# One row of w spread by a matrix product, second paths for three steps, and a new written order of all tasks

## The chip, the cores and the metric

The kernel runs on one core of one Trainium2 chip. A core has five engines that run side by side, each through its own instruction list in order: TensorE (PE, matrix products and transposes into PSUM), VectorE (DVE), ScalarE (ACT), GpSimd (POOL) and SyncE (SP, which here only issues DMAs). The metric is the device time of one execution in microseconds (us); lower is better. Three runs of the kernel before gave 139.99, 140.60 and 140.88 us, so the median is 140.60.

## The reference, cut to what matters

Two stages follow each other. The first is a linear attention with a decay `w` per head and channel and a bonus `u` for the token itself; its output is the input `x` of the second, which rotates `x` by an angle, mixes along the tokens, and then along the channels. There are B = 4 batches, H = 8 heads, S = 768 tokens and D = 48 channels a head, so x has 384 columns.

```python
for t in range(S):                                   # r, k, v: (B, H, S, D);  w, u: (H, D)
    cur = einsum('bhd,bhe->bhde', u[None] * kt, vt)
    y[:, :, t] = einsum('bhd,bhde->bhe', rt, state + cur)
    state = w[None, :, :, None] * state + einsum('bhd,bhe->bhde', kt, vt)
x = y.transpose(0, 2, 1, 3).reshape(B, S, H * D)
theta = x @ w_theta
y = einsum('ts,bsd->btd', w_tok_r, x * cos(theta)) + einsum('ts,bsd->btd', w_tok_i, x * sin(theta))
u = x + y
return u + maximum(u @ w_ch, 0)                      # (4, 768, 384) float32
```

## The kernel before, in words

Each batch is cut into three groups of 256 tokens, so there are twelve groups, g = 0 to 11 (g = 3 b + pr). `front(b)` holds the first stage and the angle for the three groups of a batch, `mixing(b)` the mixing along the tokens and channels; `setup` makes constants, and `weights` brings in the four weight matrices.

A group of `front` does the following. It loads k, r and v (L426, L432). It multiplies k and r by powers of w (tasks *kw* and *rw*, L539 and L541); those powers, `rpow` and `kpow`, are made once in `setup` by an Exp (L381) of the logarithm of w (L374). PE transposes both (*flip TK*, *flip TR*, L477, eight blocks of 128x128 each) and ACT or DVE copies the result from PSUM (*out TK*, *out TR*, L492 or L493). PE multiplies the two into scores (L585), four banks of 128x512 a group; DVE multiplies each by a 0/1 mask on its way out of PSUM (*mAT*, L594). The bonus goes by *PD* (L601), *diag* (L618), *dg* (L623) and *yd* (L627). The running state of a batch goes by *outer* (L651), then *F*, *T* and *N* (L693 to L707), with bf16 copies *Sb*. PE adds up *states*, *outputs* and *bonus* (L727, L740, L756; L779 and L792 in the last groups) and the result is copied to *x* (L764, L766, L801). *TX* transposes x, *theta* is a product of it with `w_theta` (L815), ACT takes cos and sin (L822, L826), and DVE multiplies x with both into *z* (L830). Groups 0 to 6 (`PAIRS`) hold two neighbouring tokens to a partition, groups 7 to 11 one.

A group of `mixing` has two halves t. Each half is three *mix* steps of four products (L852), one for each group of z in the batch; *un* adds x to the sum (L870, DVE, PSUM to SBUF); *TU* transposes it; *chan* is the product with `w_ch` (L884); *fin out* takes the positive part (ACT, L890, with *fin add* on POOL, L897, or DVE in one step, L893); SP writes the result out (L908, L903). The token weights must be transposed before any *mix*: POOL issues six casting loads (L446; *Wr* and *Wi* casts 0 to 2), each followed by two flips of six blocks, *flip Wr0* to *Wr5* and *flip Wi0* to *Wi5*; cast 1 feeds flips 2 and 3, cast 2 feeds flips 4 and 5. Output rows of half t in pair pr of a batch need the flips number 2 pr + t of both.

All of these are *tasks* of a `Plan`. A task lists the engines on which it can run (its *ways*), and the set of lists at the top of the file decides everything else: `ORDER` is the order in which tasks are issued, and so the order within each engine and DMA queue; `WAYS` picks each task's way; `BANKS` gives the PSUM bank of every product; `AFTER` adds ten waits of one task for another; `IDLE` puts matrix products with a zero tile, whose result nobody reads, behind a task (`unread`, L284). Such products also stand at the start (`WARM`: 6 and 8). Data dependencies are waited for besides. A transpose with a second way can be done by a DMA from SP (L483), and then its copy from PSUM falls away (way `NONE`).

At the start the tile of w, 128 equal rows, is read by one DMA of ACT (L293: `in_=rows_of(w, C)`), small tiles of w and u by two more (L388). PE's order begins: 14 zero products, the transpose of the small tile (*wu flip*, L395), flip TR0, flip TK0, flip TK2, and so on; DVE copies the small tile (*wup*, L400) before its first multiplication by a power.

Of the kernel before, what the change touches and what calls it, by code (L numbers as in the profile page):

```python
# [951 lines left out]
```

## Time and profile before

| what | value |
|---|---|
| three runs | 139.99, 140.60, 140.88 us; median 140.60 |
| profiled execution, first to last instruction (span) | 138.9 us |
| median of the runs less that span | 1.7 us |
| PE busy | 127.6 us (92%) |
| DVE, ACT, POOL busy | 107.5, 76.7, 61.7 us |
| DMA | 25.65 MB moved, 185 GB/s in the mean |

The profile gives no time of its own for the profiled execution besides the span, so sums below are made against 138.9 us, and the 1.7 us between it and the median are taken as what lies around it. A row of the view by windows shows a stretch, its length, the busy time and count of each engine, the granted TensorE clock (1.00 is full), the share of DMA and what it moved. A row of the timeline shows start, duration, engine, line, operation, what it writes and reads, and, in brackets, how long its engine had been idle and what ended that. A row of the view of DMAs ends with the time from issue to landing.

### The profile page before, as it was taken

Reading aid. Unit: us, or ns where it says so; the run is one execution under the profiler, and the core shown is the slowest. Engines: PE = TensorE matmul, PEld = TensorE weight load, DVE = VectorE, ACT = ScalarE, POOL = GpSimd, SP = SyncE. Lnnn points to the kernel's source line nnn. Section 1 sums busy time; section 2 is a strip of 40 time slices with the busy share of each in tenths; the row PEclk is TensorE's granted clock in tenths of the full one; section 3 lists DMA queues with packets and bytes.
Section 4 is the critical chain, followed back from the end, with each engine's and each line's share of the span. In section 5 each row is a group of like instructions: output and inputs, shape, how many; then the busy total and the mean of one; then the engine's idle time right before and its main releaser. Section 6 shows DMA issues by size and latency. Waiting matters only on the chain.

```text
span 138.9 us, 4469 instructions
## 1 busy us (share of the span) xinstructions
PE 127.6 (92%) x1874; PEld 85.0 (61%) x1874; DVE 107.5 (77%) x205; ACT 76.7 (55%) x145; POOL 61.7 (44%) x70
## 2 busy tenths in 40 slices
PE   0999569999996999999999999999999999999990
PEld 0334347977764767777766687577565665656640
DVE  2419397889799999999979997999699986427281
ACT  2455687799992368593898039629903133650020
POOL 5003977861041099949320199993118902002000
PEclk9999985799999999999999999999999999999999
DMA  2999999999999999739979999999972563803635
GB/s 46 250 263 263 261 225 213 210 239 211 248 254 267 261 196 147 107 67 174 193 127 267 169 217 185 147 269 187 288 177 60 103 181 87 257 0 115 114 122 218
DMA packets 67340, 25.65 MB, mean 185 GB/s; under 512 B 61816, under 2 KB 67320, under 8 KB 67320
## 3 DMA queue, kind: packets, MB, share of 16 engines
q1 hardware_dynamic: 64720, 22.22, 75.6%
q0 software_dynamic: 2432, 2.95, 12.4%
q10 hardware_dynamic: 168, 0.20, 0.7%
q8 instruction: 14, 0.23, 0.7%
q14 instruction: 6, 0.05, 0.1%
HBM read 20.25 MB, written 4.72 MB: 180 GB/s over the span
## 4 chain that ended last, share of the span: by engine, by line
PE 65%; DVE 10%; DMA 8%; POOL 6%; SPq 4%; issue 2%; ACT 2%; DVEq 0%; ACTq 0%; POOLq 0%
PE bank L852 25%; PE bank L477 9%; DMA ld<-in_v_dram 8%; PE bank L815 6%; PE bank L884 5%; PE bank L284 5%; PE bank L585 4%; POOL Kw L539 3%; PE bank L651 2%; SPq L432 2%; PE bank L740 2%; DVE Rw L539 2%; DVE PD L601 2%; PE bank L756 1%; PE bank L792 1%
## 5 line engine op out<-in xcount | busy, mean ns | idle before, releaser
L852 PE MATMUL bank<-z,WrT 128*128 128x384 bf16 x144 | 46.8, 326 | 0.0
L852 PE MATMUL bank<-z,WiT 128*128 128x384 bf16 x144 | 46.8, 326 | 0.0
L594 DVE TENSOR_TENSOR mAT<-bank,mask 128x512 bf16<-128x512 f32 x28 | 18.1, 681 | 4.3 <-PE bank L585 4.1
L539 POOL TENSOR_TENSOR Kw<-ld,kpow 128x768 bf16<-128x768 f32 x4 | 8.2, 2040 | 24.5 <-DVE Kw L539 9.9
L852 PEld LDWEIGHTS <-WrT 128*128 128x128 bf16 x144 | 14.0, 98 | 8.1
L852 PEld LDWEIGHTS <-WiT 128*128 128x128 bf16 x144 | 14.1, 98 | 8.0
L870 DVE TENSOR_TENSOR uu_all<-bank,x 128x384 bf16<-128x384 f32 x24 | 13.0, 549 | 4.9 <-PE bank L852 4.7
L826 ACT ACTIVATE trig<-bank 128x384 f16<-128x384 f32 x24 | 11.4, 504 | 7.9 <-PE bank L815 7.8
L627 POOL TENSOR_TENSOR yd<-dg,vb 128x768 bf16<-128x768 f32 x10 | 14.7, 1470 | 2.3 <-ACT lwu L403 1.3
L492 ACT ACTIVATE RT<-bank 128x1024 bf16<-128x1024 bf16 x11 | 11.3, 1026 | 6.8 <-PE bank L477 6.6
L884 PE MATMUL bank<-Wch,uu_all 128*128 128x384 bf16 x72 | 14.6, 326 | 0.1
L897 POOL TENSOR_TENSOR fin_all<-fin_all,uu_all 128x384 f32<-128x384 f32 x8 | 7.3, 913 | 16.1 <-ACT fin_all L890 14.8
L815 PE MATMUL bank<-Wth,xT 128*128 128x384 bf16 x72 | 14.3, 326 | 0.0
L284 PE MATMUL bank<-zero 128*128 128x512 bf16 x31 | 10.9, 503 | 3.6 <-DVE zero L291 3.6
L822 ACT ACTIVATE trig<-bank,pi 128x384 f16<-128x384 f32 x24 | 13.6, 594 | 0.7 <-PE bank L815 0.6
L830 DVE TENSOR_TENSOR z<-x,trig 128x1536 bf16<-128x1536 bf16 x12 | 11.7, 974 | 2.9 <-ACT trig L822 2.9
L492 ACT ACTIVATE KT<-bank 128x1024 bf16<-128x1024 bf16 x11 | 11.5, 1044 | 3.3 <-PE bank L477 3.0
L594 DVE TENSOR_TENSOR mAT<-bank,mask_c 128x512 bf16<-128x512 f32 x20 | 13.0, 681 | 0.2 <-PE bank L585 0.2
L539 POOL TENSOR_TENSOR Rw<-ld,rpow 128x768 bf16<-128x768 f32 x4 | 7.2, 1812 | 8.2 <-DVE PD L601 8.1
L893 DVE SCALAR_TENSOR_TENSOR fin_all<-bank,uu_all 128x384 f32<-128x384 f32 x16 | 8.6, 551 | 2.2 <-PE bank L884 1.8
L539 DVE TENSOR_TENSOR Rw<-ld,rpow 128x768 bf16<-128x768 f32 x8 | 9.2, 1152 | 1.0 <-DMA ld<-in_r_dram 1.0
L477 PE MATMUL bank<-ident,Kw 128*128 128x128 bf16 x96 | 7.4, 219 | 2.5 <-POOL Kw L539 2.5
(112 smaller groups left out, 219.6 us busy)
## 6 DMA issues: line engine op xcount, KB each, us to landing
ld<-in_r_dram SPq DMA_DIRECT2D x12, 384.0 KB, 6.0
out_dram<-fin_all SPq DMA_DIRECT2D x11, 384.0 KB, 3.1
ld<-in_k_dram SPq DMA_DIRECT2D x7, 384.0 KB, 10.5
ld<-in_v_dram SPq DMA_DIRECT2D x7, 384.0 KB, 6.1
ld<-in_k_dram SPq DMA_DIRECT2D x10, 192.0 KB, 4.8
ld<-in_v_dram SPq DMA_DIRECT2D x10, 192.0 KB, 5.2
z<-in_moe_w_tok_i_dram POOLq DMA_DIRECT2D x1, 384.0 KB, 7.3
fin_all<-in_moe_w_tok_r_dram POOLq DMA_DIRECT2D x1, 384.0 KB, 8.4
```

The costliest lines, as they stand in the source:

```text
L284: ins = [nc.tensor.matmul(bank_t[k][:, :wide * C].rearrange("p (a c) -> p a c", a=wide), zero, bc(zero, 1, wide), start=True, stop=True, s ...
L477: ins = [nc.tensor.matmul(bank16(tok)[:, i * C:(i + 1) * C], s, ident, is_transpose=True, start=(i == 0), stop=(i == n - 1)) for i, s in e ...
L492: ways = [act(n * C, lambda: nc.scalar.activation(dst, src(), Act.Copy)), dve(n * C, lambda: nc.vector.tensor_copy(dst, src()), 1.0 if pai ...
L539: return eng.tensor_mul(to.rearrange("p j h d -> p h j d")[:, :, :, :D], tokens(i), pw)
L594: mask01[:, j] if pairs else mask_c): nc.vector.tensor_mul(
L627: return eng.tensor_mul(yd.rearrange("p a b d -> p (a b) d"), wide(dg, D), vb.rearrange("p a b d -> p (a b) d"))
L815: ins = [nc.tensor.matmul(bank(th)[:, :HD], xT[:, t, dk, :], Wth[:, dk, :], start=(dk == 0), stop=(dk == ND - 1)) for dk in range(ND)]
L822: P.add(act(HD, lambda th=th, t=t, trig=trig: nc.scalar.activation(trig[:, t, 0], bank(th)[:, :HD], Act.Sin, bias=pi2), 144), use=[th], rd ...
L830: P.add(dve(4 * HD, lambda trig=trig, pr=pr: nc.vector.tensor_mul(z[:, 2 * pr:2 * pr + 2], bc(x[:, 2 * pr:2 * pr + 2], 2, 2), trig), 2.0, ...
L852: ins.append(nc.tensor.matmul(bank(tm)[:, :HD], (WrT, WiT)[ri][:, so, to * C:(to + 1) * C], z[:, so, ri], start=(part == 0 and i == 0), st ...
L870: P.add(dve(HD, lambda tm=tm, t=t, to=to, un=un: nc.vector.tensor_add(un[:, t], bank(tm)[:, :HD], x[:, to])), use=[tm], rd=[("x", xi, pr, ...
L884: ins = [nc.tensor.matmul(bank(tf)[:, :HD], uT[:, t, dk, :], Wch[:, dk, :], start=(dk == 0), stop=(dk == ND - 1)) for dk in range(ND)]
```

## The change

First, w: the DMA reads w as one row of 384 numbers into one partition. A new DVE task fills a row of 128 ones, and a new PE task, *spread*, multiplies the two, which puts w on all 128 partitions of a PSUM bank; the logarithm reads that bank. Spread stands behind the zero products of the start in PE's order, of which there are now six. Second, paths: a score tile can be copied out of PSUM by ACT and masked from SBUF to SBUF by DVE or POOL; a mixed sum can be copied by ACT and added to x by POOL; the transposes of k in groups 7 to 11 can be done by a DMA, for which their blocks are laid out in another order. Third, all lists are new.

```diff
-WARM, WARM_NS = (6, 8), (1280, 1700)
+WARM = 6
...
-    (69, 155), (125, 85), (156, 93), (168, 134), (249, 279), (215, 285), (232, 346), (454, 326),
-    (467, 586), (448, 633),
-]
...
+AFTER = []
 IDLE = [
-    (28, 0, 5), (73, 3, 5), (71, 3, 5), (83, 2, 1), (119, 0, 1),
+    (6, 2, 6), (74, 4, 2), (72, 5, 1), (121, 6, 1), (119, 4, 5), (91, 2, 1), (166, 6, 1), (99,
+    5, 3), (101, 4, 1),
 ]
...
-        P.add((ACT, 2950, False, lambda: nc.scalar.dma_start(out=w_row, in_=rows_of(w, C))),
+        P.add((ACT, 2950, False, lambda: nc.scalar.dma_start(
+            out=w_row[:1], in_=w.rearrange("h d -> (h d)").unsqueeze(0))),
...
+        P.add((DVE, 70, False, lambda: nc.vector.memset(one, 1.0)), wr=["one"], prio=-2e4,
+              name="one")
+
+        def spread():
+            a = nc.tensor.matmul(bank("wsp")[:, :HD], one, w_row[:1], start=True, stop=True)
+            return a, a
+        P.add(pe(640, spread), rd=["one", "w_row", "warmed"], acq=["wsp"], prio=-2e4, mode=5,
+              name="spread")
...
         P.add(act(HD, lambda: nc.scalar.activation(
-            lw_f, w_row, Act.Ln), 93), rd=["w_row", "set"], wr=["lw_f"], prio=-200,
-            name="ln")
+            lw_f, bank("wsp")[:, :HD].rearrange("p (h d) -> p h d", h=H), Act.Ln)),
+            use=["wsp"], rd=["set"], wr=["lw_f"], prio=-200, name="ln")
...
+                    P.add([(NONE, 0, False, None),
+                           act(HP * C, lambda hi=hi, tk=tk, mAT=mAT: nc.scalar.activation(
+                               mAT[:, hi], bank(tk[hi]).rearrange("p (h t) -> p h t", h=HP),
+                               Act.Copy))], use=[tk[hi]], wr=[("mAT", mi, hi)], prio=pb + 3,
+                          name="mA out", kind="mA")
...
+                           dve(HP * C, lambda hi=hi, mAT=mAT, m=m: nc.vector.tensor_mul(
+                               mAT[:, hi], mAT[:, hi], m), 2.0, True),
+                           pool(1170, lambda hi=hi, mAT=mAT, m=m: nc.gpsimd.tensor_mul(
+                               mAT[:, hi], mAT[:, hi], m))],
...
+                P.add([(NONE, 0, False, None),
+                       act(HD, lambda tm=tm, t=t, fin=fin: nc.scalar.activation(
+                           fin[:, t], bank(tm)[:, :HD], Act.Copy))], use=[tm],
+                      wr=[("fin", j, t)], prio=pb + 2 * t, name="un out", kind="un")
+                P.add([dve(HD, lambda tm=tm, t=t, to=to, un=un: nc.vector.tensor_add(
+                           un[:, t], bank(tm)[:, :HD], x[:, to])),
+                       pool(900, lambda t=t, to=to, un=un, fin=fin: nc.gpsimd.tensor_add(
+                           un[:, t], fin[:, t], x[:, to]))],
```

The new `ORDER`, `WAYS` and `BANKS`, 838 entries and more, are left out. Read off task by task they say the following. The numbers before the dot are the group, behind it the half.

- Of 48 score tiles, 28 stay on DVE alone; 20 are copied by ACT and then masked by DVE (14) or POOL (6). Of 24 sums, six go by ACT and POOL. Of the late transposes of k, groups 10 and 11 go by DMA. TX8 goes from PE to DMA, TU1 and TX4 from DMA to PE.
- The first loads come in the order r0, k0, r1, k1, k2, v0, r2, v1, v2, k3, r3 (before: r0, k0, k2, r1, k1, v0, v1, r2, v2, r3, k3).
- PE begins: six zero products, spread, six zero products, wu flip, TR0, two zero products, TK0, one, TR1, one, scores 0, TK1, five, scores 1.0, diag 0, scores 1.1, outer 0, one, diag 1, TK2, one, states 0, three, TR2, outputs 0.0, outer 1, outputs 0.1, one, scores 2, bonus 0, states 1, outputs 1, bonus 1, flips Wi2 and Wi3, TX0, TX1, diag 2, outer 2, theta 0 and 1, states 2, outputs 2, bonus 2, flips Wr3 and Wr2, TK3, TX2, mix 1.0.0, mix 1.1.0, theta 2.1, TR3, theta 2.0, mix 1.1.1, flip Wr4, scores 3, mix 1.0.1, flip Wi4, mix 1.1.2, flip Wi5, mix 1.0.2, flip Wr5; twenty tasks later flip Wi0.
- DVE begins: constants, rw0, wup, kw0, rw1, kw1, PD0, mask, three score tiles of group 0 with uw among them, PD1, then the rest of groups 0 and 1 with T0; a constant, F1, Sb (three), T1, yd1, a mask, PD2, out Wi2, vb2, two tiles of group 2, Sb, out Wi3, Sb, the third tile, kw3, z0.
- POOL begins: constants, kw2, Wi cast 1, Wth, rw2, N0, yd0, N1, Wr cast 1, two Sb, one score tile of group 2, yd2, Wr cast 2, Wi cast 2, rw3, kw5, the sum 1.0, Wi cast 0, Wr cast 0. (Before: kw2, Wi cast 2, Wth, kw1, Wr casts 2 and 1, yd0, N0, Wi cast 1, two Sb, yd1, Wr cast 0, N1, Wi cast 0, yd2.)
- At the end PE has the same last tasks (flip TU11.1, chan 9.1, flip TU11.0, chan 11.1, chan 11.0); chan 10.0 and 10.1 come among the last mix steps instead of behind them.

More of the change, by code (lines that the diff above doesn't have):

```diff
@@ L140, in issue @@
             if way[0] == NONE:
-                t.ins = self.tasks[seq - 1].ins
+                t.ins = next(d.ins for d in t.deps)
                 continue
@@ L215 @@
     zero = sb.tile([C, C], BF16, name="zero")
+    one = sb.tile([1, C], F32, name="one")
     col_i = sb.tile([C, C], mybir.dt.int32, name="col_i")
@@ L259 @@
     w_row, lw_f = [zs[1].rearrange("p o t n -> p (o t n)")[:, 2 * i * HD:2 * (i + 1) * HD]
-                   .bitcast(F32).rearrange("p (h d) -> p h d", h=H) for i in range(2)]
+                   .bitcast(F32) for i in range(2)]
+    lw_f = lw_f.rearrange("p (h d) -> p h d", h=H)
     fins = [fin_all[:, i] for i in range(3)]
@@ L289, in setup @@
     def setup():
-        if WARM:
-            P.add((DVE, 120, False, lambda: nc.vector.memset(zero, 0.0)), wr=["zero"],
-                  prio=-3e4, name="zero")
-        P.add((ACT, 2950, False, lambda: nc.scalar.dma_start(out=w_row, in_=rows_of(w, C))),
+        P.add((DVE, 120, False, lambda: nc.vector.memset(zero, 0.0)), wr=["zero"],
+              prio=-3e4, name="zero")
+        P.add((ACT, 2950, False, lambda: nc.scalar.dma_start(
+            out=w_row[:1], in_=w.rearrange("h d -> (h d)").unsqueeze(0))),
               wr=["w_row"], prio=-3e4, name="w_row", kind="small")
@@ L471, in weights, with flip @@
         cast(Wch, moe_w_ch.rearrange("(o p) n -> p o n", p=C), ["Wch"], 15, (1, 24, 87), "Wch")
-    def flip(dst, blocks, tok, prio, rd, wr, paired=False, turned=None):
+    def flip(dst, blocks, tok, prio, rd, wr, paired=False, turned=None, packets=48):
         n = len(blocks)
@@ L483, in flip @@
             ways.append(sp(lambda: nc.sync.dma_start_transpose(
-                out=turned[0], in_=turned[1].rearrange("p t n -> p (t n)")), 1450))
+                out=turned[0], in_=turned[1]), 1450))
         P.add(ways, rd=list(rd) + ["ident"], wr=wr, acq=[tok], prio=prio,
-              desc=(0, 48, 15.5) if turned else None, name="flip " + tok[0],
+              desc=(0, packets, 15.5) if turned else None, name="flip " + tok[0],
               kind="turn" if turned else "")
@@ L530, in front @@
             RT, KT, PD = (a.rearrange("p (h c q) -> p h c q", c=2, h=HP) for a in flat)
+            if not pairs:
+                KT = flat[1].rearrange("p (c h q) -> p h c q", c=2, h=HP)
             kR, kK, kRT, kKT = ("Rw", g % NR), ("Kw", g % NK), ("RT", g % NRT), ("KT", g % NKT)
@@ L550, in front @@
                       name=nm[0] + "w")
-            for to, Tw, nm, kT, kTT, two in ((KT, Kw, "TK", kK, kKT, pairs),
-                                             (RT, Rw, "TR", kR, kRT, True)):
-                to = to.rearrange("p h c q -> p h (c q)")
-                flip(to.rearrange("p h (t j) -> p h t j", j=2) if two else
-                     to.rearrange("p h (c q) -> p (h c) q", c=2),
-                     [Tw[:, j, 2 * hp:2 * hp + 2, :].rearrange("p h d -> p (h d)")
-                      for hp in range(HP) for j in range(2)], (nm, g), pb, [kT], [kTT],
-                     paired=two)
+            for to, Tw, nm, kT, kTT, two in ((flat[1], Kw, "TK", kK, kKT, pairs),
+                                             (flat[0], Rw, "TR", kR, kRT, True)):
+                blocks = [Tw[:, j, 2 * hp:2 * hp + 2, :].rearrange("p h d -> p (h d)")
+                          for j in range(2) for hp in range(HP)]
+                if two:
+                    flip(to.rearrange("p (h t j) -> p h t j", h=HP, j=2),
+                         [blocks[j * HP + hp] for hp in range(HP) for j in range(2)], (nm, g),
+                         pb, [kT], [kTT], paired=True)
+                else:
+                    to = to.rearrange("p (a q) -> p a q", q=C)
+                    flip(to, blocks, (nm, g), pb, [kT], [kTT], packets=64,
+                         turned=(to, Tw.rearrange("p j h d -> p (j h d)")))
             flat_v, flat_l = vbs[g % NV], Ls[iv]
@@ L592, in front, with pairwise @@
                 for hi in range(2):
[L593 to L601 removed]
+                    m = bc(mask01[:, j] if pairs else mask_c, 1, HP)
+                    P.add([(NONE, 0, False, None),
[3 more added lines that the diff above has]
+                          name="mA out", kind="mA")
+                    P.add([dve(HP * C, lambda hi=hi, tk=tk, mAT=mAT, m=m: nc.vector.tensor_mul(
+                               mAT[:, hi], bank(tk[hi]).rearrange("p (h t) -> p h t", h=HP), m)),
+                           dve(HP * C, lambda hi=hi, mAT=mAT, m=m: nc.vector.tensor_mul(
+                               mAT[:, hi], mAT[:, hi], m), 2.0, True),
+                           pool(1170, lambda hi=hi, mAT=mAT, m=m: nc.gpsimd.tensor_mul(
+                               mAT[:, hi], mAT[:, hi], m))],
+                          use=[tk[hi]], rd=["mask" if pairs else "mask_c"],
+                          wr=[("mAT", mi, hi)], prio=pb + 3, name="mAT", kind="mA")
+            def pairwise(eng, of=flat if pairs else (RT, KT, PD)):
+                return eng.tensor_mul(of[2], of[0], of[1])
             P.add([dve(1024, lambda f=pairwise: f(nc.vector), 2.0, True),
@@ L860, in mixing @@
                           name="mix")
-                if b * NCH + to in UN_BY_TWO:
-                    P.add(act(HD, lambda tm=tm, t=t, fin=fin: nc.scalar.activation(
-                        fin[:, t], bank(tm)[:, :HD], Act.Copy)), use=[tm],
-                        wr=[("fin", j, t)], prio=pb + 2 * t, name="un out")
-                    P.add(pool(900, lambda t=t, to=to, un=un, fin=fin: nc.gpsimd.tensor_add(
-                        un[:, t], fin[:, t], x[:, to])),
-                        rd=[("x", xi, pr, t), ("fin", j, t)], wr=[("un", j, t)],
-                        prio=pb + 2 * t, name="un add")
-                else:
-                    P.add(dve(HD, lambda tm=tm, t=t, to=to, un=un: nc.vector.tensor_add(
-                        un[:, t], bank(tm)[:, :HD], x[:, to])), use=[tm],
-                        rd=[("x", xi, pr, t)], wr=[("un", j, t)], prio=pb + 2 * t, name="un")
+                P.add([(NONE, 0, False, None),
[6 more added lines that the diff above has]
+                           un[:, t], fin[:, t], x[:, to]))],
+                      use=[tm], rd=[("x", xi, pr, t), ("fin", j, t)],
+                      wr=[("un", j, t)], prio=pb + 2 * t, name="un add", kind="un")
             single = g == B * NP - 1
```

47 lines of the change are left out of this document (18 added, 29 removed), and 86 rows, old and new, of the table ORDER.

## The prediction

> **What bounds the kernel now.** I read the page's busy times first, then the view by windows cut where PE's state changes, then PE's waits, the chain of waits and the timeline of the start.
>
> ```profile
> PE 127.6 (92%) x1874; PEld 85.0 (61%) x1874; DVE 107.5 (77%) x205; ACT 76.7 (55%) x145; POOL 61.7 (44%) x70
> L284 PE MATMUL bank<-zero 128*128 128x512 bf16 x31 | 10.9, 503 | 3.6 <-DVE zero L291 3.6
> 0.00:11.00 11.00, 7.38 (x21) 2.56 (x22) 3.75 (x25) 4.44 (x7) 2.07 (x12) 1.00 0.80 190
> 11.00:19.77 8.77, 6.25 (x123) 4.14 (x123) 5.83 (x14) 5.96 (x7) 7.21 (x6) 0.99 1.26 256
> 19.77:26.30 6.53, 6.53 (x134) 4.84 (x133) 5.51 (x11) 4.90 (x13) 4.25 (x7) 0.50 1.19 211
> 26.30:35.34 9.04, 9.00 (x211) 6.92 (x210) 7.89 (x15) 8.33 (x17) 3.96 (x5) 1.00 1.15 220
> 35.34:43.00 7.66, 6.57 (x73) 4.58 (x71) 6.76 (x8) 7.10 (x13) 2.08 (x1) 1.00 1.08 257
> 43.00:131.70 88.70, 88.39 (x1301) 60.19 (x1302) 74.06 (x130) 45.00 (x88) 42.11 (x41) 1.00 0.85 167
> ```
>
> From 43 us to the tail PE is busy for 88.39 of 88.70 us, so nothing off PE is worth anything there unless it makes PE wait. The time to be had lies ahead of the first mix step at 35.34 us. Up to there PE was busy for 7.38 + 6.25 + 6.53 + 9.00 = 29.2 us, of which 10.9 us are zero products, and the stretch at clock 0.50 did half of what it could (about 2.9 us lost on real work). So 15.4 us of useful work took 35.3 us. The rows show two more losses: 1.1 us of idle PE in the window from 35.34, and the clock.
>
> **The change part by part.** *The start.* The late links of before are here (timeline, then landings in windows of issue):
>
> ```profile
> 5.55 0.52 ACT L374 ACTIVATE z<-z 128x384 f32<-128x384 f32 x1 [1.82 <-DMA z<-in_w_dram]
> 9.77 0.16 DVE L400 COPY wup<-bank 128x4 f32<-128x4 f32 x1 [4.69 <-PE bank L395]
> 9.85 0.96 DVE L539 TENSOR_TENSOR Rw<-ld,rpow 128x768 bf16<-128x768 f32 x1
> 16.60 1.82 POOL L539 TENSOR_TENSOR Kw<-ld,kpow 128x768 bf16<-128x768 f32 x1
> 18.48 0.62 PE L477 MATMUL bank<-ident,Kw 128*128 128x128 bf16 x8 [1.69 <-POOL Kw L539]
> 5.54 1.23 SPq L426 DMA_DIRECT2D ld<-in_r_dram  x1
> ld<-in_r_dram SPq DMA_DIRECT2D x1, 384.0 KB, 5.7
> z<-in_w_dram ACTq DMA_DIRECT2D x1, 192.0 KB, 4.8
> ```
>
> Before, rw0 sits behind wup, which sits behind wu flip and 14 zero products; kw1 runs on POOL, behind kw2 and two casts, and TK1 waits for it until 18.48. After, rw0 stands ahead of wup, and kw1 is DVE's, right behind rw1. kw1 then waits only for its load, the fourth: before, the fourth was issued at 5.54 and landed 5.7 later, at 11.2. The 192 KB of w, moved at the 256 GB/s of the second window, leave the queue, which is 0.77 us: 10.5. Spread is not shown; its price on the logarithm lies between a bf16 row of the same width (0.33, the mean of the mix products) and the 4.8 us that the old DMA took. I take about 1, nearer the product, since the old logarithm began at 5.55 and the new one may begin after the table load: either way the powers are there well before the fourth load. If w lands late, each us goes on rw0.
>
> *DVE then sets the pace.* Its order from kw1 is known, and its durations are these:
>
> ```profile
> L594 DVE TENSOR_TENSOR mAT<-bank,mask 128x512 bf16<-128x512 f32 x28 | 18.1, 681 | 4.3 <-PE bank L585 4.1
> L601 DVE TENSOR_TENSOR PD<-RT,KT 128x1024 bf16<-128x1024 bf16 x10 | 7.2, 720 | 0.3 <-ACT RT L492 0.3
> L703 DVE TENSOR_TENSOR T<-bank,F 128x192 f32<-128x192 f32 x8 | 2.8, 353 | 0.3
> L627 DVE TENSOR_TENSOR yd<-dg,vb 128x768 bf16<-128x768 f32 x2 | 1.9, 948 | 0.0
> L493 DVE COPY WrT<-bank 128x768 bf16<-128x768 bf16 x4 | 2.2, 545 | 0.0
> L870 DVE TENSOR_TENSOR uu_all<-bank,x 128x384 bf16<-128x384 f32 x24 | 13.0, 549 | 4.9 <-PE bank L852 4.7
> 32.34 0.57 PE L740 MATMUL bank<-vb,mAT 64*128 64x48 bf16 x32
> 32.75 0.49 PE L756 MATMUL bank<-yd,place 64*128 64x384 bf16 x4
> ```
>
> From kw1 to T1: kw1 0.96, two PD 1.44, eight score tiles 5.45, six steps of T's kind 2.1, and mask, place and uw about 1.5, taken as four more of T's kind, in all 11.5: T1 ends at 22.0. On to the last DVE tile of group 2: yd1 0.95, PD2 0.72, three copies of 0.55, three tiles 2.0, three more of T's kind (two Sb, a mask) 1.0, in all 6.3: 28.3. Outputs 2 and bonus 2 take 0.9 behind it (32.34 to 33.24 in the trace): bonus 2 ends at 29.2 instead of 33.24. By then before had done two flips of 0.34 more and one theta of 0.49 less, so the new order is ahead by 4.0 - 0.7 + 0.5 = 3.8 us.
>
> *The casts give part of it back.* POOL issues Wr cast 1 only behind N1, which waits for T1.
>
> ```profile
> 18.36 0.76 POOL L446 DMA_DIRECT2D fin_all<-in_moe_w_tok_r_dram  x1
> fin_all<-in_moe_w_tok_r_dram POOLq DMA_DIRECT2D x1, 384.0 KB, 8.4
> L627 POOL TENSOR_TENSOR yd<-dg,vb 128x768 bf16<-128x768 f32 x10 | 14.7, 1470 | 2.3 <-ACT lwu L403 1.3 <-ACT dg L623 0.7
> L706 POOL TENSOR_TENSOR N<-T,w 128x192 f32<-128x192 f32 x5 | 2.5, 500 | 2.6 <-DVE T L703 1.7 <-DVE PD L601 0.9
> L897 POOL TENSOR_TENSOR fin_all<-fin_all,uu_all 128x384 f32<-128x384 f32 x8 | 7.3, 913 | 16.1 <-ACT fin_all L890 14.8 <-ACT xT L492 1.3
> L764 ACT ACTIVATE x<-bank 128x384 bf16<-128x384 f32 x11 | 5.1, 493 | 3.7 <-PE bank L756 3.6
> 35.50 0.65 PE bank L852 x4
> 36.15 0.49 PE bank L815 x3
> 36.64 0.45 PE bank L477 x8
> 37.57 0.68 PE bank L477 x12
> 28.56 0.38 PE bank L585 x16
> ```
>
> Before, the first Wr cast was issued at 18.36; now it is at 22.0 + 0.5 = 22.5 and lands 8.4 later, at 30.9. PE stands at flip Wr3 from 29.2: 1.7 lost, 2.1 ahead. Wr cast 2 is issued behind the POOL score tile and yd2. The tile's copy stands on ACT behind x of group 1, which waits for yd1 (23.0): bonus 0.5, two x of 0.49, a copy of about 0.6, then a POOL tile of about 1.1, so 26.2; dg2 stands behind two transpose copies on ACT, near 26.9; yd2 takes 1.47; cast 2 is issued at 28.4 and lands at 36.8. PE, from 30.9, has four flips' worth of short work (0.68 + 0.45 + 0.34 + 0.45), three mix steps and two theta, 4.85 together: it stands at flip Wr4 from 35.75, 1.05 lost, 1.1 ahead. Wi cast 0 is issued behind the sum 1.0, which needs mix 1.0.2: 36.8 + three flips, two scores and three mix steps is 40.6, ACT's copy 0.49 and POOL's addition 0.91 make 42.0, and it lands 8.4 later, at 50.4. PE reaches flip Wi0 after 9.4 more of such work (five flips and six mix steps are two thirds of it), at 50.0: another 0.4. So 0.7 ahead.
>
> *Later stretches.* The idle 1.1 us of before is this:
>
> ```profile
> 40.29 2.57 DVE L539 TENSOR_TENSOR Rw<-ld,rpow 128x768 bf16<-128x768 f32 x1
> 39.96 2.08 POOL L539 TENSOR_TENSOR Kw<-ld,kpow 128x768 bf16<-128x768 f32 x1 [8.12 <-DMA ld<-in_k_dram]
> 42.91 0.62 PE L477 MATMUL bank<-ident,Rw 128*128 128x128 bf16 x8 [1.09 <-DVE Rw L539]
> ```
>
> The DVE multiplication took 2.57 beside POOL's instead of 0.96. kw6 goes to DVE, so this place goes: +1.1. TK10, TK11 and TX8 leave PE, TU1 and TX4 come back: 0.9 + 0.34 - 0.68 is +0.56. The second paths take 20 x 0.68 + 6 x 0.55 = 16.9 us from DVE and give 14 masks of 0.36 (half a PD; at most a tile's 0.68) back; but four kw, two yd, four fin out (each 0.55 like a sum), five Sb and three transpose copies come to DVE, 3.8 + 1.9 + 2.2 + 1.8 + 1.6 = 11.3, so its total falls by 16.9 - 5.0 - 11.3 = 0.6 only. A POOL tile lies between 0.98 (yd by size) and 1.47, an ACT copy between 0.49 and twice that; ACT has room beside its 76.7 us. In the tail PE's last steps are the same: 0.
>
> The 14 masks and all POOL tiles now read only SBUF, where the pair above stood in each other's way. The Trainium skill, SBUF — State Buffer, Who interferes with whom, calls the shared port of DVE and GpSimd an exclusive lock, held for a whole instruction. By that rule, with POOL busy 44% of the time, a mask would meet it about every second time and wait up to a microsecond, some 5 us more of DVE; by the sum above it is nothing, and PE's 99.7% would have to absorb it. The 2.57 us agrees with the lock.
>
> Sum: 0.7 + 1.1 + 0.5 = 2.3 us off 138.9, span 136.6; with the 1.7 us between span and median, 138.3. An unforeseen wait in the steady stretch would come off that; the old order has 0.3 us of idle PE in 88.7, so I count none.
>
> **The rivals.** *No waits on casts (G).* With less in the DMA queues at 22 us than at 18 the casts land sooner than 8.4 us, and 2.8 of the 3.15 us that the waits cost (1.7 + 1.05 + 0.4) stay: 135.5. Against it: the DMA share is over 1.0 in all windows from 11 to 43 us.
>
> *The clock falls again (C).* Before, PE was idle for 2.5 of the 8.77 us ahead of 19.77, and then the clock stood at 0.50 until 26.3. The new order waits for DVE tiles in the same stretch, with 27 zero products in all against 31. If the clock halves again while PE bounds, the same 2.9 us are lost: 138.3 + 2.9 = 141.2, no change. The Trainium skill, TensorE: Matmul & The Clock Gate, Part 4, says that transposes do not count as PE work for the gate. By that rule the eight-block transposes of the start keep nothing warm; the trace agrees only so far that the clock fell although PE was busy for 6.25 of 8.77 us.
>
> *The last casts come late (S), slower.* The last cast was issued at 28.93 before (below); now the last two stand on POOL behind an addition that needs a finished mix, and by the sum above there is no slack: every microsecond is PE's. A load that met the casts took 13.0:
>
> ```profile
> ld<-in_k_dram SPq DMA_DIRECT2D x1, 384.0 KB, 13.0
> 28.93 0.76 POOL L446 DMA_DIRECT2D x<-in_moe_w_tok_i_dram  x1
> ```
>
> 13.0 in place of 8.4 is 4.6 us: 142.9. Slower than 142.0 it is from 3.7 us on. For it: no wait of `AFTER` is kept, and order on POOL alone sets it. Against: DMA traffic may have thinned by 42 us.
>
> *It does not do what it says (N).* DVE and POOL lock each other as above and the new lists stall PE where the old did not, by as much as the casts left: 140.6.
>
> **How the numbers follow.** One per cent, 1.4 us, is about what a measurement of this kernel can tell from no change. The forecast has 0.42 and its own range, 136.5 to 139.2; G 0.14; C 0.13; N 0.12; S 0.19. Faster than 139.2: 0.42 + 0.14 = 0.56. Within 1%: C and N, 0.25. Slower: 0.19. The range reaches down into G, to 134.3, and up past C and N to 141.9, just short of S, which leaves out about two in ten.
>
> **What would show it.** In the changed profile: kw1 on DVE at 10.5 to 11.5 and TK1 before 13; T1 near 22 and bonus 2 near 29; PE idle at flips Wr3, Wr4 and Wi0 with the DMA as releaser, 1.7, 1.05 and 0.4 us; no 1.1 us idle by rw5; the window after 53 us as full as before. If PE is not idle at these flips, G holds; if the clock's slices show 5 between 14 and 26 us, C; if flip Wi0 waits 3 us or more, S; idle PE after 53 us with DVE or POOL as releaser, N. The prediction is wrong at its root if useful PE work by 35 us is not above 15.4.

## The result and the profile after

The changed kernel is slower: 145.16 us (median of four runs, 144.84 to 146.57) against 140.62 us for the kernel before, run beside it. The ratio is 1.036, with an interval of 1.030 to 1.041. The forecast was 138.3 us with a range of 134.3 to 141.9, so the sign is wrong and the time lies outside the range. Medians here and below are of all runs of a kernel, while ratios and intervals leave out runs more than 1.5% above its fastest, so the two can differ a little. The profiled execution of the changed kernel spans 143.1 us, 4.2 us more than the 138.9 of before.

The page of the changed kernel shows where to look: busy times, PE and its clock in 40 slices of 3.6 us, and the chain of waits by engine.

```profile
PE 128.6 (90%) x1862; PEld 82.9 (58%) x1862; DVE 116.2 (81%) x211; ACT 85.0 (59%) x163; POOL 60.8 (43%) x68
PE   7989797790999999896999999999999999999990
PEclk9999999999599999999999999999999999999998
PE 55%; DVE 20%; ACT 9%; DMA 7%; issue 5%; POOL 1%; POOLq 0%; DVEq 0%; ACTq 0%
```

PE is only 1.0 us busier than before, but its row has a hole (a 0 in the tenth slice, about 32 to 36 us) and behind it the clock is at half. DVE grew from 107.5 to 116.2 us, although its total was forecast to fall by 0.6. The same stretches by windows (length, busy time of PE, PEld, DVE, ACT and POOL with counts, granted clock, DMA share, GB/s):

```profile
20.00:32.28 12.28, 10.36 (x259) 7.70 (x253) 11.00 (x22) 10.20 (x20) 8.22 (x10) 1.00 1.18 258
32.28:36.06 3.78, 0.00 (x0) 0.00 (x1) 3.78 (x3) 1.26 (x2) 2.43 (x2) 0.99 1.18 218
36.06:39.40 3.34, 3.34 (x11) 1.60 (x12) 1.74 (x3) 0.00 (x0) 0.00 (x0) 0.50 1.19 284
...
53.00:135.50 82.50, 80.27 (x1122) 52.97 (x1118) 69.34 (x121) 47.22 (x96) 36.44 (x36) 1.00 0.77 158
```

Three losses stand in these rows: 1.92 us of idle PE before 32.28, 3.78 us with PE quite still and 3.34 us at clock 0.50 behind it, and 2.23 us spread over the rest (82.50 less 80.27), where the old order had 0.31 in 88.70. The timeline has the instructions, PE, DVE and POOL mixed in order of time; a bracket tells how long the engine had been idle, and for what:

```profile
10.20 0.95 DVE L552 TENSOR_TENSOR Kw<-ld,kpow 128x768 bf16<-128x768 f32 x1
21.67 0.34 DVE L728 TENSOR_TENSOR T<-bank,F 128x192 f32<-128x192 f32 x1
23.23 0.76 POOL L457 DMA_DIRECT2D uu_all<-in_moe_w_tok_r_dram  x1
25.97 0.22 PE L488 MATMUL bank<-ident,fin_all 128*128 128x128 bf16 x1 [1.81 <-issue]
30.23 0.49 PE L781 MATMUL bank<-yd,place 64*128 64x384 bf16 x4
30.40 0.72 POOL L457 DMA_DIRECT2D z<-in_moe_w_tok_i_dram  x1
30.43 5.10 DVE L855 TENSOR_TENSOR z<-x,trig 128x1536 bf16<-128x1536 bf16 x1
31.14 1.82 POOL L552 TENSOR_TENSOR Rw<-ld,rpow 128x768 bf16<-128x768 f32 x1
32.91 1.80 POOL L552 TENSOR_TENSOR Kw<-ld,kpow 128x768 bf16<-128x768 f32 x1
36.06 0.50 PE L877 MATMUL bank<-z,WrT 128*128 128x384 bf16 x1 [3.79 <-DVE WrT L504]
...
63.42 2.15 DVE L618 TENSOR_TENSOR mAT<-mAT,mask 128x512 bf16<-128x512 bf16 x1
63.79 1.49 POOL L652 TENSOR_TENSOR yd<-dg,vb 128x768 bf16<-128x768 f32 x1
67.11 0.43 PE L676 MATMUL bank<-vb,Kw 64*64 64x48 bf16 x24 [1.26 <-DVE xT L504]
```

The start went as forecast: kw1 on DVE at 10.20 (10.5 was forecast), T1 ends at 22.01 (22.0). Then PE stood for 1.81 us without any releaser ("issue"), so bonus 2 ends at 30.72 instead of 29.2. And then came the largest loss. z0, an elementwise product of two SBUF tiles that takes 0.95 us elsewhere, took 5.10 us, beside rw3 and kw5 on POOL, and ended 0.82 us behind them. The first mix step needs z0 and the copies of Wr queued behind it on DVE, so PE had nothing to do for 3.79 us, and the clock halved. At 63 us a mask of 0.41 us took 2.15 beside yd5 on POOL; PE waited 1.26 us for the copy two places behind it. Over all, by groups (busy us, mean ns):

```profile
L855 DVE TENSOR_TENSOR z<-x,trig 128x1536 bf16<-128x1536 bf16 x12 | 15.9, 1322 | 3.1 <-ACT trig L847 2.8 <-ACT trig L851 0.3
L618 DVE TENSOR_TENSOR mAT<-mAT,mask 128x512 bf16<-128x512 bf16 x7 | 5.5, 786 | 0.0
L618 DVE TENSOR_TENSOR mAT<-mAT,mask_c 128x512 bf16<-128x512 bf16 x7 | 2.9, 420 | 0.8 <-ACT mAT L612 0.8
```

In the kernel before, z took this:

```profile
L830 DVE TENSOR_TENSOR z<-x,trig 128x1536 bf16<-128x1536 bf16 x12 | 11.7, 974 | 2.9 <-ACT trig L822 2.9
```

Of the 8.7 us by which DVE grew, the products z make 4.2 (15.9 less 11.7), nearly all of it z0.

### The profile page after: what moved, and what is told of

Its sections match the earlier page's. It is cut to its first block, busy times and chain, and to the rows that moved or that the text cites. A ratio compares the mean times of both kernels' runs of the same rounds, so it can differ in the third digit from the quotient of the medians.

```text
span 143.1 us, 4466 instructions
## 1 busy us (share of the span) xinstructions
PE 128.6 (90%) x1862; PEld 82.9 (58%) x1862; DVE 116.2 (81%) x211; ACT 85.0 (59%) x163; POOL 60.8 (43%) x68
## 4 chain that ended last, share of the span: by engine, by line
PE 55%; DVE 20%; ACT 9%; DMA 7%; issue 5%; POOL 1%; POOLq 0%; DVEq 0%; ACTq 0%
PE bank L877 24%; PE bank L907 7%; DMA xT<-x 7%; PE bank L840 6%; PE bank L488 5%; DVE z L855 4%; DVE mAT L616 4%; DVE PD L626 3%; ACT RT L503 2%; DVE mAT L618 2%; PE bank L291 2%; PE bank L676 2%; PE bank L602 2%; ACT KT L503 2%; DVE Kw L552 1%
## 5 line engine op out<-in xcount | busy, mean ns | idle before, releaser
L855 DVE TENSOR_TENSOR z<-x,trig 128x1536 bf16<-128x1536 bf16 x12 | 15.9, 1322 | 3.1 <-ACT trig L847 2.8
L652 POOL TENSOR_TENSOR yd<-dg,vb 128x768 bf16<-128x768 f32 x8 | 12.1, 1516 | 11.6 <-ACT dg L648 11.6
L890 DVE TENSOR_TENSOR uu_all<-bank,x 128x384 bf16<-128x384 f32 x18 | 9.8, 551 | 7.1 <-PE bank L877 6.8
L892 POOL TENSOR_TENSOR uu_all<-fin_all,x 128x384 bf16<-128x384 f32 x6 | 6.8, 1134 | 18.2 <-ACT fin_all L887 18.2
L612 ACT ACTIVATE mAT<-bank 128x512 bf16<-128x512 f32 x20 | 11.6, 602 | 2.9 <-PE bank L602 2.8
L920 POOL TENSOR_TENSOR fin_all<-fin_all,uu_all 128x384 f32<-128x384 f32 x4 | 3.6, 912 | 18.8 <-ACT fin_all L913 18.8
L616 DVE TENSOR_TENSOR mAT<-bank,mask 128x512 bf16<-128x512 f32 x17 | 11.0, 679 | 0.1
L626 DVE TENSOR_TENSOR PD<-RT,KT 128x1024 bf16<-128x1024 bf16 x11 | 9.4, 858 | 0.5 <-ACT RT L503 0.3
L840 PEld LDWEIGHTS <-xT 128*128 128x128 bf16 x72 | 6.4, 99 | 5.6 <-DMA xT<-x 1.5
L907 PEld LDWEIGHTS <-uu_all 128*128 128x128 bf16 x72 | 6.7, 98 | 4.5 <-ACT uu_all L503 0.4
```

The costliest lines, as they stand in the source:

```text
L612: act(HP * C, lambda hi=hi, tk=tk, mAT=mAT: nc.scalar.activation(mAT[:, hi], bank(tk[hi]).rearrange("p (h t) -> p h t", h=HP), Act.Copy))] ...
L616: P.add([dve(HP * C, lambda hi=hi, tk=tk, mAT=mAT, m=m: nc.vector.tensor_mul(mAT[:, hi], bank(tk[hi]).rearrange("p (h t) -> p h t", h=HP), ...
L626: return eng.tensor_mul(of[2], of[0], of[1])
L652: return eng.tensor_mul(yd.rearrange("p a b d -> p (a b) d"), wide(dg, D), vb.rearrange("p a b d -> p (a b) d"))
L840: ins = [nc.tensor.matmul(bank(th)[:, :HD], xT[:, t, dk, :], Wth[:, dk, :], start=(dk == 0), stop=(dk == ND - 1)) for dk in range(ND)]
L855: P.add(dve(4 * HD, lambda trig=trig, pr=pr: nc.vector.tensor_mul(z[:, 2 * pr:2 * pr + 2], bc(x[:, 2 * pr:2 * pr + 2], 2, 2), trig), 2.0, ...
```

## The experiments

The theory after these rows: the new order is no worse in its work, but it puts multiplications of POOL beside those products of DVE on which PE waits, and they shut DVE out. The old order had ten waits in `AFTER`; the new one has none. Rivals: the second paths cost more than they bring; the half clock is the loss; the one-row w gives nothing; the new order is slower for other reasons. Ratios below are to the kernel before, run beside each.

| kernel | median, us | ratio (interval) |
|---|---|---|
| after | 145.16 | 1.036 (1.030 to 1.041) |
| after, two waits | 142.69 | 1.013 (1.004 to 1.022) |
| before, no waits | 144.25 | 1.027 (1.021 to 1.033) |
| after, zero products | 145.16 | 1.035 (1.027 to 1.044) |
| after, w as 128 rows | 148.29 | 1.052 (1.042 to 1.062) |
| after, two waits, one path | 145.87 | 1.040 (1.035 to 1.045) |
| after, four waits | 141.95 | 1.012 (1.007 to 1.017) |
| after, three waits | 141.41 | 1.009 (1.004 to 1.014) |
| after, two waits, late load | 141.94 | one run |
| after, three waits, late load | 139.93 | 0.996 (0.991 to 1.000) |
| before, one-row w | 138.80 | 0.991 (0.988 to 0.995) |
| before, one-row w, z2 first | 137.41 | 0.981 (0.972 to 0.991) |
| the same, kw1 on DVE | 138.01 | 0.985 (0.978 to 0.992) |

**Two waits.** rw3 starts only after z0, kw5 only after z1.

```diff
-AFTER = []
+AFTER = [(113, 207), (160, 300)]     # rw3 after z0, kw5 after z1
```

> The changed kernel with two waits put back: POOL's rw3 waits for z0, POOL's kw5 waits for z1. Lock theory: z0 took 5.10 us instead of 0.95 because rw3 and kw5 ran on POOL at that time, both engines multiplying SBUF by SBUF; with the waits z0 takes under 1.3 us, PE's idle 3.8 us ahead of the first mix step shrinks below 1 us, the clock does not fall at 36 us, and the kernel takes 139.8 to 141.2 us. Rival (cast theory): the long z0 comes from the casting load issued at 30.40, which stays: z0 stays near 5 us and the kernel near 145. Second rival (next wait): the stall goes but flip Wr4 then waits for its cast, and under 2 us is won, 143 or more.

```profile
31.22 0.96 DVE L855 TENSOR_TENSOR z<-x,trig 128x1536 bf16<-128x1536 bf16 x1 [0.74 <-ACT trig L847]
33.61 0.34 PE L877 MATMUL bank<-z,WrT 128*128 128x384 bf16 x1
```

142.69 us. z0 takes 0.96 us, PE no longer waits ahead of the first mix, and that comes 2.45 us sooner. So it was the overlap with POOL's work that made z0 late, and it cost about 2.5 of the 4.5 us that the change lost (3.2 by the ratios). In this run z0 starts when POOL is through with issuing the cast as well (30.37 to 31.09 us), so this run alone can't tell the cast from the multiplications; the kernel under "All of it", below, does. The clock fell in this run too, at 27 us, behind the stall without a releaser.

**The old kernel without its waits.** `AFTER` of before is emptied, nothing else.

```diff
-AFTER = [(69, 155), (125, 85), ..., (448, 633)]
+AFTER = []
```

> The kernel before with its ten extra waits taken out, nothing else. Lock theory: these waits kept POOL's SBUF work off DVE's; without them DVE's excess over its shortest durations grows from 2.5 us to 5 or more and the kernel loses 1 to 4 us, 141.6 to 144.6. Rival: the waits are leftovers, kw2 and its casts come earlier, and the time stays within 0.7 us of 140.6.

```profile
12.72 0.62 PE L474 MATMUL bank<-ident,Kw 128*128 128x128 bf16 x8 [1.21 <-DVE Kw L536]
17.83 0.46 PE L648 MATMUL bank<-vb,Kw 64*64 64x48 bf16 x32 [1.40 <-ACT vb L558]
29.18 0.43 PE L648 MATMUL bank<-vb,Kw 64*64 64x48 bf16 x16 [1.39 <-DVE vb L560]
39.76 1.82 POOL L536 TENSOR_TENSOR Kw<-ld,kpow 128x768 bf16<-128x768 f32 x1 [7.61 <-DMA ld<-in_k_dram]
40.52 1.87 DVE L827 TENSOR_TENSOR z<-x,trig 128x1536 bf16<-128x1536 bf16 x1
42.45 0.32 PE L849 MATMUL bank<-z,WrT 128*128 128x384 bf16 x1 [0.76 <-DVE z L827]
```

144.25 us, 4 us slower than with them: in the old order the ten waits were worth about as much as the change lost. Only a part of it is the same picture. z beside a multiplication on POOL takes 1.87 us and PE waits 0.76, and kw0 beside kw2 makes PE wait 1.21. But PE also waits 1.40 and 1.39 us for copies of v, the second of which waits for its load. And most of the loss lies in the head: from 47.00 to 135.50 us PE is idle for 1.04 us, where with the waits it was 0.31 in a stretch about as long.

**Zero products in the gap.** Fifteen products with the zero tile stand behind flip TX2, where PE waits for z0, so that the clock holds.

```diff
-    5, 3), (101, 4, 1),
+    5, 3), (101, 4, 1), (194, 6, 15),
```

> The changed kernel with 15 more zero products behind flip TX2, in the 3.8 us in which PE stood idle. The stall itself stays. Clock theory: the granted clock stays at 1.00 from 36 to 39.5 us instead of 0.50, worth half of 3.4 us: 143.4 to 143.9. Rival: the clock cost nothing because DVE was the bound there, 144.8 to 145.6.

Windows of this kernel and then of the changed one:

```profile
36.00:40.00 4.00, 3.93 (x40) 2.66 (x44) 3.26 (x6) 1.85 (x4) 0.00 (x0) 1.00 1.10 274
100.00:120.00 20.00, 18.76 (x242) 12.03 (x240) 16.00 (x30) 9.02 (x20) 6.18 (x7) 1.00 0.98 199
```

```profile
36.00:40.00 4.00, 3.94 (x20) 2.10 (x21) 1.80 (x4) 0.25 (x1) 0.00 (x0) 0.57 1.18 278
100.00:120.00 20.00, 19.82 (x249) 12.72 (x247) 16.87 (x33) 10.41 (x24) 7.77 (x9) 1.00 0.83 192
```

145.16 us, the same. The clock stayed at 1.00 (0.57 without the products) and PE did twice the instructions from 36 to 40 us, but from 100 to 120 us it now stood still for 1.24 us (20.00 less 18.76; 0.18 without). At 65 us PE was still 1.68 us ahead (65.43 against 67.11 for the same product). The half clock behind the hole is real, but removing it won nothing that these runs show: what it gave was taken back by later waits.

**w as 128 rows again.** One DMA brings 128 rows, the logarithm reads that tile, one zero product stands in place of spread; all else as changed.

```diff
-            a = nc.tensor.matmul(bank("wsp")[:, :HD], one, w_row[:1], start=True, stop=True)
-            return a, a
+            return unread(P.bank_of["wsp"], 1)
...
-            out=w_row[:1], in_=w.rearrange("h d -> (h d)").unsqueeze(0))),
+            out=w_row.rearrange("p (h d) -> p h d", h=H), in_=rows_of(w, C))),
```

> The changed kernel with w read as 128 rows again and the logarithm taken from that tile; the product that spread w is replaced by one zero product. Theory (as predicted): 192 KB more in the queue put every early load 0.77 us later, so kw1, T1 and the first mix step come 0.5 to 0.8 us later: 145.6 to 146.0. Rival: rw0 waited for the powers and not for loads, the spread took 1.6 us of PE and won nothing: 144.8 to 145.4.

```profile
7.79 0.20 PE L405 MATMUL bank<-ident_f,wu 8*128 8x8 f32 x1 [2.02 <-DMA wu<-in_w_dram]
11.29 0.96 DVE L551 TENSOR_TENSOR Kw<-ld,kpow 128x768 bf16<-128x768 f32 x1 [0.49 <-DMA ld<-in_k_dram]
```

148.29 us, 3.1 more than the changed kernel (2.3 by the ratios). I had priced the one row at 0.77 us, its bytes. PE's wait of 2.02 us for the small load of w costs nothing by itself: the flip behind it ran no later than in the changed kernel (7.79 against 7.91), and the next one needs rw0, which started 0.30 us later (7.82 against 7.52). What the 128 rows hold back is the loads of k. SP issued that of k1 at 5.55 us instead of 2.98; kw1 then waits for it and starts at 11.29 instead of 10.20, and kw2 on POOL starts at 12.91 instead of 10.62. By T1 the delay is 3.0 us (how it grew so far was not taken apart), and the first mix came at 39.35 us instead of 36.06.

**One path.** The kernel with two waits, and every mask and sum read from PSUM by DVE again, at the place of its copy.

```diff
-WAYS = (... mA out 1, mAT 1 or 2; un out 1, un 1 ...)     # 20 masks, 6 sums
+WAYS = (... mA out 0, mAT 0;      un out 0, un 0 ...)     # each product moved to its copy's place in ORDER
```

> The two-wait kernel (142.7 us) with every second path undone: all 28 mask products and all 18 mix sums are read from PSUM by DVE again, each product put where its copy through ACT stood; 20 copies and 6 sums' copies leave ACT, 6 masks and 6 sums leave POOL. In the two-wait profile DVE is 112.3 us busy; a mask from PSUM is 677 ns, one from SBUF 784 and 452 ns (their mean is 0.62), a sum from PSUM 550 ns: DVE gains about 6 x 0.68 + 14 x 0.06 + 6 x 0.55 = 8.2 us to 120.5. Theory R (the second paths relieve DVE, and it needs that): slower by 1.5 to 4 us, PE waits for masks and sums from DVE. Theory W (the second paths only put work beside DVE that blocks it, and what they relieve was idle): within 1 us of 142.7, DVE's excess over the shortest durations falls from 5.9 to under 4 us, and the wait of 1.26 us for the xT copy near 64 us goes.

```profile
66.26 0.61 PE L486 MATMUL bank<-ident,Rw 128*128 128x128 bf16 x8 [1.01 <-DVE mAT L614]
```

145.87 us, 3.2 more than with the second paths: PE waits for masks and copies on DVE. The second paths are worth what they do in this order, and are not what made it slow.

**Four waits and three waits.** To the two waits are added: kw2 after PD0, and yd5 after mask 5.1.1; then the second alone.

```diff
-AFTER = [(113, 207), (160, 300)]
+AFTER = [(113, 207), (160, 300), (87, 164), (316, 320)]     # four
+AFTER = [(113, 207), (160, 300), (316, 320)]                # three
```

> The two-wait kernel (142.7 us, span 140.7) with two more waits: kw2 on POOL starts after PD0 on DVE (they overlapped at 11.8 us, PD0 1.59 instead of 0.67), and yd5 on POOL starts after mask 5.1.1 on DVE (2.15 instead of 0.41 us; the xT copy behind it holds PE for 1.26 us at 64.5). Theory L (what is left of the loss is such collisions, and PE has no other limit behind them): PD0 0.67, the mask 0.41 to 0.5, the idle time at 64.5 gone, 141.2 to 141.6 us. Theory G (a time won in the middle is given back at later transfers, as with the zero products): the idle time at 64.5 goes, but that before the transposes by DMA near 95 and 100 us grows by as much, 142.3 to 142.8 us.

> The two-wait kernel with only the second of the two waits added in the four-wait one (142.0 us): yd5 on POOL after mask 5.1.1 on DVE; kw2 is free again. Theory L (that mask's 1.74 us is what the four waits won, and holding kw2 back for PD0 cost part of it): the idle time of 1.26 us at 64.5 goes, 141.3 to 141.8 us. Theory G (it is given back at later transfers): 142.3 to 142.8 us.

```profile
60.44 0.41 DVE L618 TENSOR_TENSOR mAT<-mAT,mask 128x512 bf16<-128x512 bf16 x1
```

141.95 and 141.41 us. The mask takes 0.41 us (the row is of three waits) and the wait of 1.26 us is gone in both. By the medians that is 0.7 to 1.3 us, but the intervals overlap with that of two waits, so the size is uncertain; whether holding kw2 back costs anything can't be told from the two.

**The stall without a releaser.** The records of DMA packets show a queue of the kind "instruction" with packets of 16 KB; whose instructions they are they don't say. The second packet ended at 24.53 us in the changed kernel, and PE went on at 25.97. In every kernel here that shows the stall, PE went on 1.3 to 1.5 us behind that packet's end, and in every one it stopped behind 350 weight loads and 349 or 350 products, whatever these were. The kernel before came to that place at 28.53 us, 1.3 us behind the end of its packet, and had no stall. To test it, the load of k5, and with it all later loads on SP, waits for bonus 1.

```diff
-    136, 93, 167, 99, 95, 126, 297, 123, ...  250, 172,
+    136, 93, 167, 99, 95, 126, 123, ...  297, 250, 172,
-AFTER = [(113, 207), (160, 300)]
+AFTER = [(113, 207), (160, 300), (149, 297)]     # load k5 after bonus 1
```

> The two-wait kernel of the new order (142.7 us) with the load of k5, and so all loads behind it on SP, held back until the products of bonus 1 on PE have ended (about 23 us; they were issued from 15.1 us on). Theory F (the stall of 1.77 us at 25.9 without a releaser is PE's instruction packet queued behind these loads): the packet ends 1 us or more sooner and the stall is under 0.7 us; the first mix starts at 32 to 33 us instead of 33.6; what the later loads cost afterwards is open, 141 to 145 us. Rival (the stall has another cause): it stays at 1.5 to 1.9 us.

The window from 20.00 to 24.50 of the kernel with two waits, then that window and three lines of the timeline of this one:

```profile
20.00:24.50 4.50, 4.09 (x140) 2.90 (x135) 4.42 (x14) 4.17 (x7) 2.68 (x5) 1.00 1.22 271
```

```profile
20.00:24.50 4.50, 4.25 (x144) 3.06 (x139) 4.42 (x14) 4.18 (x7) 2.68 (x5) 1.00 0.52 106
```

```profile
23.48 1.00 SPq L437 DMA_DIRECT2D ld<-in_k_dram  x2
24.33 0.22 PE L488 MATMUL bank<-ident,fin_all 128*128 128x128 bf16 x1 [0.17 <-issue]
31.29 0.34 PE L877 MATMUL bank<-z,WrT 128*128 128x384 bf16 x1
```

With the DMA share at 0.52 instead of 1.22 the packet ended 1.5 us sooner, the stall shrank from 1.77 to 0.17 us, the clock held, and the first mix came at 31.29 instead of 33.61. So the stall comes from the loads, and what fits it is PE's instruction packet queued among them. The one run of 141.94 us lies within the runs of two waits; PE now waits for casts instead.

**All of it.** Three waits and the late load.

```diff
-AFTER = []
+AFTER = [(113, 207), (160, 300), (316, 320), (149, 297)]     # and 297 moved ahead of 250 in ORDER
```

> The new order with all that the runs have singled out: rw3 after z0, kw5 after z1, yd5 after mask 5.1.1, and the load of k5 after bonus 1. Theory S (the loss is these three things: z0 behind rw3 and kw5, the mask behind yd5, PE's instructions behind the loads; each was worth 2.5, 1.3 and 0.6 us when taken away, 4.4 together of the 4.5 to 4.9 by which the new order lies behind the old): 140.3 to 141.1 us, as the kernel before. Theory H (the 2.3 us forecast as gain are in there as well, and come out once the three are gone): 138 to 139 us. Theory G (the time won is given back at casts and transfers): 141.2 to 141.9 us.

```profile
29.00 0.72 POOL L457 DMA_DIRECT2D z<-in_moe_w_tok_i_dram  x1
29.03 0.95 DVE L855 TENSOR_TENSOR z<-x,trig 128x1536 bf16<-128x1536 bf16 x1
35.15 0.51 PE L488 MATMUL bank<-ident,fin_all 128*128 128x128 bf16 x6 [0.87 <-DMA fin_all<-in_moe_w_tok_r_dram]
37.58 0.51 PE L488 MATMUL bank<-ident,z 128*128 128x128 bf16 x6 [0.59 <-DMA z<-in_moe_w_tok_i_dram]
50.73 0.84 PE L488 MATMUL bank<-ident,z 128*128 128x128 bf16 x12 [0.73 <-DMA z<-in_moe_w_tok_r_dram]
...
47.00:130.00 83.00, 80.68 (x1157) 53.15 (x1157) 68.14 (x122) 48.11 (x98) 36.48 (x36) 1.00 0.93 171
```

139.93 us, at most 1% faster than before, or the same. Against three waits alone (ratio 1.009; the intervals don't meet) the late load is worth 1.5 us by the medians and 1.9 by the ratios. Taking away these collisions and most of the instruction packet's delay (the stall is 0.80 us here) takes away the whole loss, but brings out no gain of 2.3 us. Three things are to be seen. z0 runs in 0.95 us though it starts, as in the changed kernel, while POOL issues a cast; what differs is that rw3 does not follow. So issuing the cast did not shut z0 out, and the multiplications behind it did. Waits of PE's flips for casts now appear, 0.87 for Wr cast 2, 0.59 for Wi cast 2 and 0.73 for Wr cast 0 (2.19 together); in the changed kernel the hole at z0 had covered them. I had forecast 1.7 for Wr cast 1, which does not show, 1.05 for Wr cast 2 and 0.4 for Wi cast 0. And from 47 to 130 us PE is still idle for 2.32 us.

**The one-row w in the old order.** The first part alone: one row, spread in place of the second set of zero products (which follow it), rw0 ahead of wup, six zero products of the start dropped.

```diff
-            lw_f, w_row, Act.Ln), 93), rd=["w_row", "set"], ...
+            lw_f, bank("wsp")[:, :HD].rearrange("p (h d) -> p h d", h=H), Act.Ln), 93), use=["wsp"], ...
-    13, 109, 22, 28, 21, 29, 70, 24, ...
+    13, 109, 22, 28, 21, 70, 29, 24, ...
```

> The kernel before (140.1 us) with the first part of the change alone: w loaded as one row and spread by a product in place of the 8 zero products of the second warm-up (these come behind it), the logarithm read from the bank; rw0 ahead of the copy of w and u in DVE's list, 3 of the 5 zero products ahead of TR0 and of TK0 dropped. Lists, engines and waits otherwise as before. By the profile of after, rw0 starts at 7.5 instead of 9.85 us, kw0 at 8.5 instead of 11.56. Theory P (the old order is bound by PE and DVE from there on): 2.0 to 3.0 us of it reach the end, 137.1 to 138.1 us. Theory Q (the lead is used up where the old order waits for loads and for K on POOL, as far as the first mix at 35.3 us): the first mix comes less than 1 us earlier and the time is 139.3 to 140.3 us.

```profile
38.13 1.82 POOL L546 TENSOR_TENSOR Kw<-ld,kpow 128x768 bf16<-128x768 f32 x1 [7.10 <-DMA ld<-in_k_dram]
38.47 2.29 DVE L837 TENSOR_TENSOR z<-x,trig 128x1536 bf16<-128x1536 bf16 x1
40.81 0.32 PE L859 MATMUL bank<-z,WrT 128*128 128x384 bf16 x1 [1.18 <-DVE z L837]
```

138.80 us, between the two theories: faster than before. The lead of the start met the same two traps, a stall of 1.74 us without a releaser at 27 us and z2 beside kw6 on POOL. The profiled run is the slowest of the ten (139.99). And the edit is more than w: rw0's place and six zero products less are in the 1.2 us that it won (140.03 to 138.80).

**z2 ahead of kw6, and kw1 on DVE.** One wait more, kw6 after z2. Then also kw1 on DVE right behind rw1, with kw2 waiting for kw1.

```diff
-    (467, 586), (448, 633),
+    (467, 586), (448, 633), (189, 368),     # kw6 after z2
```

> The old order with the one-row w (138.8 us) and one wait more: kw6 on POOL starts after z2 on DVE. In the profile without the wait z2 took 2.29 instead of 0.95 us beside kw6 (38.13 to 39.95), and PE stood still for 1.18 us at 40.8. Theory L (the lock at z is a loss by itself): z2 0.95 to 1.0 us, no idle time of PE over 0.4 us there, 137.4 to 138.0 us. Theory G (kw6 comes 1.3 us later, and PE waits for its transposes instead): 138.5 to 139.2 us.

> As the last, and kw1 on DVE instead of POOL, right behind rw1 and ahead of the clearing of Sd, with kw2 on POOL waiting for kw1 instead of kw0. The wait of 1.69 us for kw1 at 16.9 us goes. The other stall of the head, 1.74 us without a releaser at 27.3, is put down to the fetch of PE's instructions: it ended 1.44 to 1.50 us behind the end of the second 16 KB packet of that queue in every run. Theory L (a lead in the head reaches the end): 135.7 to 136.6 us, the stall at 27 still about 1.7. Theory F (that packet comes no sooner, so the stall takes the lead up): the stall grows to 2.5 us or more and the time is 137.0 to 138.2 us.

One row is of the kernel with z2 first, and the next of that with kw1 on DVE:

```profile
39.30 0.95 DVE L837 TENSOR_TENSOR z<-x,trig 128x1536 bf16<-128x1536 bf16 x1
```

```profile
13.43 0.62 PE L484 MATMUL bank<-ident,Kw 128*128 128x128 bf16 x8 [1.88 <-POOL Kw L546]
```

137.41 us with z2 first: 1.9% faster than the kernel before, and the best of all kernels here. z2 takes 0.95 us and PE has no wait there. Its interval overlaps with that of the one row alone, and its profiled start was also luckier (0.64 us of instruction stall instead of 1.74), so I don't put all of the 1.4 us down to the wait. kw1 on DVE brings nothing more (138.01): the wait for kw1 only turned into a wait of 1.88 us for kw2, which stands behind it. The instruction stall did not grow to 2.5 us or more, as one theory had it, but was 0.91.

## Why the prediction was wrong, point by point

**Right: the start.** The DVE order gave T1 at 22.0, and it was 22.01; kw1 10.5 against 10.20. Some of that is luck: kw1 followed rw1 without waiting for its load, and PD0 took 2.12 us beside kw2 instead of 0.72, which shorter steps behind it made up for. That the wait at rw5 goes (+1.1) held as well. Wr cast 1 was issued at 23.23 (22.5 in the sum). By the sign that the prediction calls its root, the order was barely ahead: by 35.34 us PE had been busy for 27.49 us, 10.05 of them zero products and 1.64 the spread, which leaves 15.8 of useful work against 15.4.

**Mis-sized: the one-row w.** "The 192 KB of w ... which is 0.77 us" counted bytes. Undoing it cost 3.1 us in the new order (2.3 by the ratios), by the loads that it holds back; in the old order it won 1.2 us together with rw0's place and fewer zero products.

**Missed: bonus 2 at 29.2.** It ended 1.5 us late, by the stall put down to PE's instruction packet, which no step had. With two waits and the late load it ended at 29.27, as the sum had it. The new order reached the place of the stall in PE's list some 4 us sooner than the old one, and so before the packet had come.

**Right in kind, covered: "The casts give part of it back".** In the changed kernel PE did not stand at the flips, because it stood at z0 instead. With z0 freed and the load held back, such waits cost 2.19 us instead of the 3.15 of the sum, at other flips in part.

**The step that failed** is the end of "Later stretches", and with it the paragraph on the lock. "The 14 masks and all POOL tiles now read only SBUF" weighed the lock for the masks alone, and "An unforeseen wait in the steady stretch would come off that; the old order has 0.3 us of idle PE in 88.7, so I count none" took the old order's fullness for the new one's. No step priced z beside POOL's multiplications, although z too multiplies two SBUF tiles and the first mix waits for it. The change dropped the waits in `AFTER`, and I had read that as a fact for the casts only (rival S); without them the old order loses 4 us too, though mostly ahead of its steady stretch and only in part by such collisions. The runs put in place of "none": about 2.5 us at z0 in the head, some 0.7 to 1.3 us at a mask, and 2.2 us of idle time after 53 us, of which that mask's 1.26 is part. The masks themselves came to 8.4 us (5.5 + 2.9) against 5.0 in the sum; the price of "some 5 us" that the rule would give them was 3.4, and it mattered only where PE waited at once.

The Trainium skill, SBUF — State Buffer, Who interferes with whom, says that a VectorE instruction with two SBUF inputs contends with a GpSimd instruction that reads SBUF, while one with at most one SBUF input, outside the two-port modes, does not, and that the shared ports are an exclusive lock. The traces agree on the sorting: the 28 masks that read PSUM took 673 to 692 ns in every case, while z, PD and the SBUF masks, with two SBUF inputs, went from 0.94 to 5.10 us, from 0.67 to 2.12 and from 0.41 to 2.15. So the rule covered z0 as it covered the masks; I quoted half of it.

**The rivals.** N was the mechanism ("the new lists stall PE where the old did not"), at a chance of 0.12 and a price that kept it at no change; a price worked out from the longest step that PE waits for (z0 behind two POOL multiplications of 1.8 us) would have been some 4 us, and on the slower side. S, the slower rival that I chose, did not decide: the last two casts cost 0.34 us (two waits) and 0.73 (all of it) where they showed. C came true as a sight, the clock at 0.50 from 36 to 39 us, but holding the clock won nothing.

**What stays open.** With these causes gone, the last in most part, the new order is 0.6 us ahead of the old at the median (140.55 beside it), where the forecast had 2.3. The 2.32 us of idle PE from 47 to 130 us is enough to hold the difference, but was not taken apart further. Nor is it settled what z0 did in the 0.71 us between its start and that of rw3; the mask at 63 us likewise started 0.37 us ahead of yd5, while POOL issued a load, and ended 0.29 behind it.
